# Weight loads that write 128 rows, gate and up blocks paired, and a new order in a one-core attention and feed-forward kernel

## Chip, core and metric

The kernel runs on one core of a Trainium2 chip. The metric is the time of one execution on the device in microseconds (us). The kernel before has a median of 236.81 us over three runs (236.5 to 237.31).

## What is computed

The input x has 2048 rows of 448 numbers (bf16). Its rows are normalised, and the normalised xn feeds two branches. The reference, cut to what matters:

```
xn = layernorm(x)
# branch A: attention in 4 segments of 512 rows, 16 heads of 28, with a memory from segment to segment
q, k, v = xn @ wq, xn @ wk, xn @ wv
for s in range(4):
    p   = softmax(q_s @ k_s.T * 28**-0.5 + causal mask)
    o_s = g * (phi(q_s) @ M) / (phi(q_s) @ z + 1e-6) + (1 - g) * (p @ v_s)
    M  += phi(k_s).T @ v_s ;  z += sum(phi(k_s))
s = o @ wo
# branch B: feed-forward, 448 -> 1792 -> 448
b = (gelu(xn @ w_gate) * (xn @ w_up)) @ w_down
out = x + s * silu(b)
```

## The kernel before, in words

The work goes by segments of 512 rows, in the order attention 0, gate and up 0, attention 1, gate and up 1, and so on; the down product of a segment is done during the attention of the next. 448 is three and a half times 128, so each contraction over 448 is cut into seven chunks of 64 rows. TensorE works on two 64-row halves at once: a matmul on rows 0 to 63 and one on rows 64 to 127 alternate, for two different outputs. Therefore each weight that is contracted with xn stands twice over: in `wqk_sb` wq lies in rows 0 to 63 and wk in rows 64 to 127; in `wgu_sb` the gate weights lie in rows 0 to 63 and the up weights in rows 64 to 127. xn, transposed, is kept in two tiles: `xnT`, and `xS` with the two halves exchanged (`swapped`, L709 and L711: two DMAs from SBUF to SBUF).

`gate_up` (L1183 on) makes one block of 128 hidden columns at a time, 14 blocks a segment: 14 matmuls (L1195), eight that read `xnT` and then six that read `xS`, alternately for the gate bank and the up bank. ScalarE then applies gelu (L1200) and VectorE multiplies by the up bank into `hT` (L1205).

The loads are written with `load` (L592), each one DMA instruction on the queue of SyncE (SP) or ScalarE (ACT). They come in this order: x of segment 0 (`x0`), wq and wk, x of segment 1 (`x1`), wv, x of segment 2 (`x2`), then gate and up in six pieces (L616): four, four and six blocks, each piece 64 rows by 7 chunks by 512 or 768 columns. Later come `wo_in` (L658, 28 rows each) and w_down (L666, 128 rows).

SP also issues all other transfers of the kernel: the DMA transposes of q, k (L870) and xn (L801), the `xS` exchanges, and the transfers that spread the softmax denominators (`den` L998, `dc` L1029, `rdr` L1038, `rb` L1043). SP works in order: an instruction that waits holds those behind it. Each DMA takes one of eight landing semaphores in turn, so it also waits for the landing of the DMA eight before it.

The order on every engine is made when the kernel is built: `arrange` (L371) plays the operations through with estimated durations, picks by the numbers of a table (`PRIO`, and `STEP`, which ties an operation to a step of the attention), and so also decides PSUM banks and who evicts them.

Some names: `wd_sb` holds w_down later, and at first the k and v of segment 0; `kT` and `qT` are the transposed k and q; `pt` are the exponentials of the scores (L1112 ScalarE, scores L1097, product with v L1159); `up0` (L972) is the memory update of segment 0.

Of the kernel before, what the change touches and what calls it, by code (L numbers as in the profile page):

```python
# [1813 lines left out]
```

## Time and profile before

| | |
|---|---|
| median of three runs | 236.81 us |
| the profiled execution: its own time | 237.62 us |
| its span, first to last instruction | 235.9 us |
| mean granted TensorE clock | 0.992 |
| TensorE (PE) busy | 219.2 us, 93% |
| ScalarE (ACT), VectorE (DVE), GpSimd (POOL) busy | 164.9, 157.3, 130.3 us |
| TensorE idle from 0 to 60 us of the span | 10.5 us |
| TensorE busy from 80 to 220 us | 140.0 of 140 us |
| moved by DMA | 27.48 MB, mean 116 GB/s |

The span is what the trace covers; 1.7 us of the execution's time lie around it. The DMA share is the time that packets took, over the 16 DMA engines; it can exceed 1 when packets of one engine overlap. SPq in a row is SP issuing a transfer; where such a row is long, the instruction was held. A DMA's own time is not in that row.

### The profile page before, as it was taken

To read this page: it belongs to the slowest core of one execution; us is meant where nothing else is said; L and a number is where in the kernel's file an instruction comes from. 1 tells how busy PE (TensorE), PEld (TensorE's weight loads), DVE (VectorE), ACT (ScalarE), POOL (GpSimd) and SP (SyncE) were. 2 spreads that over 40 slices of the span, in tenths; PEclk is the share of its full clock that TensorE was granted. 3 is DMA by queue.
4 is the path that set the end of the run, shared out by engine and by line. 5 is a ranking of instruction groups with operands and counts; after the bars stand their busy time and mean duration, and the time that the engine had idled before them with its cause. 6 is when DMAs were issued, how large, how long until landed. Compare 5 with 4: busy or idle time off the path is not lost.

```text
span 235.9 us, 5509 instructions
## 1 busy us (share of the span) xinstructions
PE 219.2 (93%) x2084; PEld 102.8 (44%) x2084; DVE 157.3 (67%) x289; ACT 164.9 (70%) x224; POOL 130.3 (55%) x225
## 2 busy tenths in 40 slices
PE   7786799699999999999999999999999999999990
PEld 4443345244444454444444444445544444445560
DVE  4489499746636998479785676556757795556453
ACT  5596987969469977894397977994769885345120
POOL 5344599600008799971737865314899788054600
PEclk9999999999999999999999999999999999999996
DMA  6999999969940372332669513419056002177011
GB/s 168 227 212 126 189 156 178 165 123 203 262 91 10 68 183 47 90 107 56 167 152 157 144 29 89 76 36 202 27 154 164 3 8 71 47 201 181 1 42 43
DMA packets 43543, 27.48 MB, mean 116 GB/s; under 512 B 28232, under 2 KB 38920, under 8 KB 43512
## 3 DMA queue, kind: packets, MB, share of 16 engines
q1 hardware_dynamic: 42616, 26.43, 55.5%
q10 hardware_dynamic: 896, 0.66, 1.0%
q8 instruction: 17, 0.28, 0.5%
q14 instruction: 14, 0.11, 0.3%
HBM read 16.23 MB, written 2.98 MB: 81 GB/s over the span
## 4 chain that ended last, share of the span: by engine, by line
PE 74%; DMA 7%; SPq 5%; ACT 5%; DVE 4%; issue 2%; POOL 0%; DVEq 0%; ACTq 0%
PE ps L1195 16%; PE ps L1231 16%; PE pp L1195 15%; PE ps L826 11%; PE pp L1097 5%; ACT pt L1112 4%; PE ps L1261 4%; PE ps L1159 4%; DMA x_sb<-in_A_x_dram 4%; SPq L870 3%; DMA wgu_sb<-in_B_w_up_dram 3%; PE ps L1010 1%; PE ps L972 1%; SPq L801 1%; DVE st L750 1%
## 5 line engine op out<-in xcount | busy, mean ns | idle before, releaser
L1112 ACT ACTIVATE pt<-pp 128x1024 bf16<-128x1024 f32 x75 | 73.1, 1028 | 15.5 <-PE pp L1097 15.3
L1123 POOL TENSOR_SCALAR_AFFINE_SELECT pt<-pt 128x256 bf16<-128x256 bf16 x128 | 54.7, 455 | 42.0 <-ACT pt L1112 41.4
L1195 PEld LDWEIGHTS <-wgu_sb 64*128 64x128 bf16 x784 | 38.7, 94 | 49.0 <-issue 4.9
L1231 PE MATMUL ps<-wd_sb,hT 128*128 128x448 bf16 x210 | 43.7, 353 | 0.0
L1195 PE MATMUL pp<-xnT,wgu_sb 64*128 64x512 bf16 x224 | 30.6, 376 | 0.4 <-DMA wgu_sb<-in_B_w_up_dram 0.3
L1195 PE MATMUL ps<-xnT,wgu_sb 64*128 64x512 bf16 x224 | 30.2, 376 | 0.0
L1205 DVE TENSOR_TENSOR hT<-gl,ps 128x512 bf16<-128x512 bf16 x28 | 18.7, 682 | 17.2 <-ACT gl L1200 17.2
L1200 ACT ACTIVATE gl<-pp 128x512 bf16<-128x512 f32 x28 | 16.5, 598 | 19.1 <-PE pp L1195 19.1
L1205 DVE TENSOR_TENSOR hT<-gl,pp 128x512 bf16<-128x512 bf16 x28 | 18.9, 682 | 14.9 <-ACT gl L1200 14.5
L1231 PEld LDWEIGHTS <-hT 128*128 128x128 bf16 x210 | 19.1, 98 | 19.6 <-issue 4.1
L1021 POOL TENSOR_TENSOR om<-om,rb 128x512 f32<-128x512 f32 x12 | 14.8, 1263 | 21.5 <-DMA rb<-rdr 21.5
L1195 PE MATMUL pp<-xS,wgu_sb 64*128 64x512 bf16 x168 | 24.7, 376 | 2.1 <-DMA xS<-xnT 2.1
L1200 ACT ACTIVATE gl<-ps 128x512 bf16<-128x512 f32 x28 | 16.4, 598 | 12.8 <-PE ps L1195 12.1
L1195 PE MATMUL ps<-xS,wgu_sb 64*128 64x512 bf16 x168 | 24.1, 376 | 0.0
L1068 POOL TENSOR_TENSOR oT<-oa,om 128x512 bf16<-128x512 f32 x12 | 15.4, 1294 | 7.9 <-DVE oa L1065 7.9
L943 POOL TENSOR_SCALAR e<-e 128x896 bf16<-128x896 bf16 (+1 forms) x12 | 12.4, 1037 | 9.8 <-ACT e L938 9.4
L826 PE MATMUL ps<-wqk_sb,xnT 64*128 64x448 bf16 x116 | 15.2, 351 | 1.8 <-DMA wqk_sb<-in_A_wk_dram 1.1
L995 DVE COPY oa<-ps 128x512 f32<-128x512 f32 x16 | 10.7, 685 | 6.2 <-PE ps L1159 5.4
L826 PEld LDWEIGHTS <-xnT 64*128 64x128 bf16 x192 | 8.9, 94 | 12.9 <-issue 6.3
L1252 POOL TENSOR_TENSOR oo<-sg,x_sb 128x448 bf16<-128x448 f32 x12 | 13.3, 1115 | 0.3 <-POOL e L943 0.2
L1097 PE MATMUL pp<-qT,kT 32*128 32x384 bf16 (+3 forms) x186 | 12.9, 300 | 0.2 <-ACT pt L1112 0.2
L1261 PE MATMUL ps<-wo_sb,oT 128*128 128x448 bf16 x52 | 11.7, 353 | 0.0
(134 smaller groups left out, 316.5 us busy)
## 6 DMA issues: line engine op xcount, KB each, us to landing
rb<-rdr SPq DMA_DIRECT2D x28, 256.0 KB
xS<-xnT SPq DMA_DIRECT2D x14, 192.0 KB
out_dram<-oo SPq DMA_DIRECT2D x15, 112.0 KB
wd_sb<-in_B_w_down_dram SPq DMA_DIRECT2D x2, 784.0 KB
x_sb<-in_A_x_dram SPq DMA_DIRECT2D x3, 448.0 KB
wgu_sb<-in_B_w_gate_dram SPq DMA_DIRECT2D x2, 448.0 KB
wgu_sb<-in_B_w_up_dram SPq DMA_DIRECT2D x2, 448.0 KB
rdr<-dc SPq DMA_DIRECT2D x28, 32.0 KB
```

The source lines that it names most:

```text
L826: nc.tensor.matmul(out=self.bank.ap()[:, 0:D], lhsT=chunk(self.xT, self.xt, h, self.hi)[:, n * P:(n + 1) * P], rhs=self.w[side[self.hi], h ...
L1021: oU[s, g, 1] = t, gps(f"sm{s}{g}", 1.22, lambda t=t, r=r: nc.gpsimd.tensor_tensor(out=t.ap(), in0=t.ap(), in1=r.ap(), op=ALU.mult), deps= ...
L1068: oT[s][1].append(gps(f"cb{s}{g}", 1.22, lambda g=g, t=t, tm=tm: nc.gpsimd.tensor_tensor(out=dst.ap()[:, g, :], in0=t.ap(), in1=tm.ap(), o ...
L1097: nc.tensor.matmul(out=S2[i // 2].ap(i % 2)[:, c0:c0 + n], lhsT=kT[s][0].ap()[r, g, kb * P:(kb + 1) * P], rhs=qT[s][0].ap()[r, g, kb * P:L ...
L1112: nc.scalar.activation(out=dst, in_=src, func=ACT.Exp, scale=scale)
L1123: nc.gpsimd.affine_select(out=v, in_=v, pattern=[[0, 2], [1, P]], compare_op=ALU.is_ge, fill=0.0, base=0, channel_multiplier=-1)
L1195: nc.tensor.matmul(out=bf.ap(i), lhsT=wgu_sb[side[i], h, cols], rhs=chunk(xT, xt, h, i), start=k == 0, stop=k == NH - 1)
L1200: a = act(f"ge{s}{fc}", L, lambda bf=bf, gl=gl: nc.scalar.activation(out=gl.ap(), in_=bf.ap(0), func=ACT.Gelu_apprx_tanh), func="gelu", de ...
L1205: nc.vector.tensor_tensor(out=hT[s][0].ap()[:, fc, :], in0=gl.ap(), in1=bf.ap(1), op=ALU.mult), deps=[a] + held,
L1231: nc.tensor.matmul(out=bank.ap()[:, 0:D], lhsT=hT[s][0].ap()[:, fc, b * P:(b + 1) * P], rhs=wd_sb[:, fc, :], start=(fc == 0), stop=(fc == ...
L1252: o = op(f"fa{s}{b}{h}", eng, lambda: (nc.vector if o.on == "DVE" else nc.gpsimd).tensor_tensor(out=oo.ap()[:, r], in0=t.ap()[:, r], in1=x ...
L1261: nc.tensor.matmul(out=bank.ap()[:, 0:D], lhsT=oT[s][0].ap()[:, g, b * P:(b + 1) * P], rhs=wo_sb[:, g, :], start=(g == 0), stop=(g == G - 1))
```

## The change

Seven things are changed.

1. The gate and up weights get a tile each, `wg_sb` and `wu_sb`, of 7 chunks by 896 columns. Rows 0 to 63 hold hidden blocks 0 to 6, rows 64 to 127 blocks 7 to 13. One load brings one 64-row chunk of one weight for all 1792 columns: it writes 128 rows of 896 columns (224 KB). There are 14 such loads, in turn gate and up.
2. `gate_up` makes block f and block f+7 of the gate together, then the same two of up. A gate product therefore needs all seven gate loads, where before the first four blocks needed only the first gate piece and the first up piece.
3. wv is loaded in two transfers of 128 rows by three chunks and two of 64 rows by one chunk. Its chunks stand one place further in the lower half of the rows (`(h - self.hi) % NH`), and its product needs all four loads.
4. wq and wk are written with one loop; what is loaded, by which queue and in which order stays as it was.
5. The planner starts its engines at `BEGIN` rather than at 0, and has other estimates for loads, for the check of the norms (`nrm`, `nrm2`) and for `ca`.
6. Each half of a gate or up product has a bank of its own to choose, where before gate and up of a block took a pair of banks.
7. `PRIO` and `STEP` are new throughout, and with them the order on every engine.

```diff
+BEGIN = {"PE": 0.9, "ACT": 0.82, "DVE": 0.93, "POOL": 0.8, "SP": 0.81}
...
-    "wd_in1": 469, "wg0": 310, "wg4": 308, "wg8": 128, "wk0": 445, "wk1": 753, "wo0": 668,
...
-    free = {e: 0.0 for o in ops for e in o.eng}
+    free = dict(BEGIN)
...
-        wgu_sb = const.tile([P, NH, F], BF16, name="wgu_sb")
+        wg_sb = const.tile([P, NH, F // 2], BF16, name="wg_sb")
+        wu_sb = const.tile([P, NH, F // 2], BF16, name="wu_sb")
...
-        wv_in = weight("SP", "wvl", wv_sb, 0, A_wv, [slice(0, NH)]) + weight("SP", "wvh", wv_sb, 1, A_wv, [slice(0, NH)])
+        wv_in = [load("SP", f"wv{k}", wv_sb[:, k:2 * NC3:2, :], A_wv[k * HALF:k * HALF + NC3 * P, :].rearrange(
+            "(c p) n -> p c n", p=P), 336) for k in range(2)]
+        wv_in += [load("SP", f"wv{i + 2}", wv_sb[side[i], NH - 1, :], A_wv[r, :], 56) for i, r in enumerate(
+            (slice(NC3 * P, D), side[0]))]
...
-        gu_in = []
-        for lo, hi in ((0, 4), (4, 8), (8, NFC)):
-            r = slice(lo * P, hi * P)
-            gu_in += [[load("SP", f"{n}{lo}", wgu_sb[side[i], :, r], ap[:, r].rearrange(
-                "(c p) n -> p c n", p=HALF), 112 * (hi - lo)) for i, (n, ap) in enumerate((
-                    ("wg", B_w_gate), ("wu", B_w_up)))]] * (hi - lo)
+        wg_in, wu_in = [], []
+        for h in range(NH):
+            for to, w, ap in ((wg_in, wg_sb, B_w_gate), (wu_in, wu_sb, B_w_up)):
+                to.append(load("SP", f"{'gu'[to is wu_in]}w{h}", w[:, h, :], ap[h * HALF:(h + 1) * HALF, :].rearrange(
+                    "p (i n) -> i p n", i=2), 224, 0.6))
...
+                    prev = pe(f"{'gu'[j]}g{s}{f}", [L] * NH, mm, mode="r64", deps=xd + xe + (wg_in, wu_in)[j],
+                              after=[prev or att.get("sc_end")], prio=at(ph, 2 * f + j) + 0.5, acq=bs, uses=[xT, xt])
```

In the access pattern of the new gate and up loads (`"p (i n) -> i p n"`) the DRAM side counts 2, then 64, then 896 columns; the SBUF side counts 128 rows of 896.

The first place is SP's queue from the load of `x2` on. Before (`wd_sb<-wd_sb` are the transposes of the k of segment 0 into `kT`; `xS_97` is the exchange for the projections of segment 1):

```order
L592 DMA x_sb_65<-in_A_x_dram 128x4x448
L592 DMA wgu_sb<-in_B_w_gate_dram 64x7x512
L592 DMA wgu_sb<-in_B_w_up_dram 64x7x512
L870 DMA_TRANSPOSE wd_sb<-wd_sb 128x4x128 x3
L709 DMA xS_97<-xnT_94 64x1536
L711 DMA xS_97<-xnT_94 64x1536
L592 DMA wgu_sb<-in_B_w_gate_dram 64x7x512
L801 DMA_TRANSPOSE xnT_95<-xn_92 128x4x128 x2
```

After, the same queue from the fifth gate or up load to the exchange `xS_98` for segment 1, with the semaphore that each waits for:

```order
L596 DMA wg_sb<-in_B_w_gate_dram 128x1x896 [waits DMAHW1_49]
L596 DMA wu_sb<-in_B_w_up_dram 128x1x896 [waits DMAHW2_49]
L596 DMA wg_sb<-in_B_w_gate_dram 128x1x896 [waits DMAHW3_49]
L876 DMA_TRANSPOSE wd_sb<-wd_sb 128x4x128 [waits DMAHW4_49,Activation_49,Pool_49]
L876 DMA_TRANSPOSE wd_sb<-wd_sb 128x4x128 [waits DMAHW5_49,Activation_49]
L596 DMA wu_sb<-in_B_w_up_dram 128x1x896 [waits DMAHW6_49]
L876 DMA_TRANSPOSE wd_sb<-wd_sb 128x4x128 [waits DMAHW7_49,DVE_49]
L596 DMA wg_sb<-in_B_w_gate_dram 128x1x896 [waits DMAHW0_49]
L596 DMA wu_sb<-in_B_w_up_dram 128x1x896 [waits DMAHW1_49]
L664 DMA wo_sb<-in_A_wo_dram 28x4x448 [waits DMAHW2_49,Pool_49]
L664 DMA wo_sb<-in_A_wo_dram 28x4x448 [waits DMAHW3_49]
L715 DMA xS_98<-xnT_95 64x1536 [waits DMAHW4_49,DVE_49]
```

Before, two gate and up pieces stand ahead of the three transposes; now seven loads do, and three more stand ahead of the exchange for segment 1.

The second place is the same queue, later. Before, from the last gate piece to the first `den` (the last up piece comes after eight more transposes and an exchange, not shown):

```order
L592 DMA wgu_sb<-in_B_w_gate_dram 64x7x768
L870 DMA_TRANSPOSE qT_98<-e_103 128x4x128
L709 DMA xS_96<-xnT_95 64x1536
L711 DMA xS_96<-xnT_95 64x1536
L998 DMA den_149<-oa_112 4x512
```

After, from the last three gate and up loads to the exchange `xS_97`, which the gate and up of segment 0 read:

```order
L596 DMA wg_sb<-in_B_w_gate_dram 128x1x896
L807 DMA_TRANSPOSE xnT_96<-xn_93 128x4x128 x3
L596 DMA wu_sb<-in_B_w_up_dram 128x1x896
L807 DMA_TRANSPOSE xnT_96<-xn_93 128x4x128
L596 DMA betac<-in_A_beta_dram 128x1x1
L664 DMA wo_sb<-in_A_wo_dram 28x4x448
L715 DMA xS_97<-xnT_96 64x1536
L717 DMA xS_97<-xnT_96 64x1536
```

Now every gate and up load stands ahead of this exchange, and the last of them ahead of the fourth transpose of xn.

The third place is TensorE around its first gate product. Before (`pp1_87` is a pair of banks):

```order
L972 MATMUL ps3_91<-wd_sb_72 128x128
...
L1159 MATMUL ps2_90<-pt0_106,wd_sb_72 32x512
...
L1097 MATMUL pp0_86<-hT_81,wd_sb_72 128x384
...
L1195 MATMUL pp1_87<-xnT2_95,wgu_sb_71 128x512
...
L1195 MATMUL pp1_87<-xS0_96,wgu_sb_71 128x512
```

After:

```order
L1103 MATMUL ps1_90<-hT_82,wd_sb_73 128x128
...
L1203 MATMUL pp1_88<-xnT2_96,wg_sb_71 128x512
...
L1203 MATMUL pp1_88<-xS0_97,wg_sb_71 128x512
...
L978 MATMUL ps0_89<-wd_sb_73 128x128
...
L1165 MATMUL ps3_92<-pt0_107,wd_sb_73 32x512
```

The memory update `up0` (L978) and a product with v (L1165) stood ahead of the gate products and now stand behind the first three of them. The sum of TensorE's rows is the same (5627).

More of the change, by code (lines that the diff above doesn't have):

```diff
@@ L445, in fast_path @@
     NFC = F // P
+    FH = NFC // 2
     NC3 = D // P
@@ L589, in fast_path, with load @@
         first = []
-        def load(eng, name, dst, src, kb, rate=320.0):
-            o = op(name, {eng: (0.5, 2.0)}, lambda: (nc.sync if eng == "SP" else nc.scalar).dma_start(
-                out=dst, in_=src), after=first[-1:], prio=-1000, kb=kb, rate=rate)
+        def load(eng, name, dst, src, kb, occ=0.68):
+            o = op(name, {eng: (occ, 1.45)}, lambda: (nc.sync if eng == "SP" else nc.scalar).dma_start(
+                out=dst, in_=src), after=first[-1:], prio=-1000, kb=kb, rate=335.0)
             first.append(o)
@@ L597, in fast_path, with rows64 @@
         side = slice(0, HALF), slice(HALF, P)
-        def weight(eng, name, dst, hi, ap, parts):
-            v = ap.rearrange("(c p) n -> p c n", p=HALF)
-            return [load(eng, f"{name}{k or ''}", dst[side[hi], c, :], v[:, c, :], len(range(*c.indices(NH))) * ap.shape[1] / 8, 300.0)
-                    for k, c in enumerate(parts)]
-        x0 = [load(e, f"x0{lo}", xs[0][:, lo:hi, :], x_v[0][:, lo:hi, :], 112 * (hi - lo))
+        def rows64(ap):
+            return ap.rearrange("(c p) n -> p c n", p=HALF)
+        x0 = [load(e, f"x0{lo}", xs[0][:, lo:hi, :], x_v[0][:, lo:hi, :], 112 * (hi - lo), 0.45)
               for e, lo, hi in (("SP", 0, 1), ("ACT", 2, 4), ("SP", 1, 2))]
@@ L826, in product @@
                 nc.tensor.matmul(out=self.bank.ap()[:, 0:D], lhsT=chunk(self.xT, self.xt, h, self.hi)[:, n * P:(n + 1) * P],
-                                 rhs=self.w[side[self.hi], h, :], start=k == 0, stop=k == NH - 1)
+                                 rhs=self.w[side[self.hi], (h - self.hi) % NH if self.nm == "wv" else h, :], start=k == 0, stop=k == NH - 1)
             def out(self, o):
@@ L892, in pair @@
             else:
-                f = pe(name, [D] * NC3, mm(0, NC3), deps=[u.w_in[0], v.w_in[0]] + xd, prio=pr, **kw)
-                o = pe("r" + name, [D] * (NH - NC3), mm(NC3, NH), mode="r64", deps=[f, u.w_in[1], v.w_in[1]] + xe,
+                f = pe(name, [D] * NC3, mm(0, NC3), deps=(u.w_in if u.nm == "wv" else [u.w_in[0], v.w_in[0]]) + xd, prio=pr, **kw)
+                o = pe("r" + name, [D] * (NH - NC3), mm(NC3, NH), mode="r64", deps=[f, u.w_in[-1], v.w_in[-1]] + xe,
                        prio=pr - 0.5, uses=[u.bank, v.bank, u.xT])
@@ L1185, in gate_up @@
             (xT, xd), (xt, xe) = xnT[s], xS[s, "g"]
-            hT[s] = [Buf(hT_p), []]
-            prev = a = None
-            for fc in range(NFC):
-                bf, cols = Buf(B_, ANY), slice(fc * P, (fc + 1) * P)
-                def mm(bf=bf, cols=cols):
-                    for k in range(NH):
-                        for i in range(2):
-                            h = turn_of[i][k]
-                            nc.tensor.matmul(out=bf.ap(i), lhsT=wgu_sb[side[i], h, cols], rhs=chunk(xT, xt, h, i),
-                                             start=k == 0, stop=k == NH - 1)
-                o = prev = pe(f"gu{s}{fc}", [L] * 7, mm, mode="r64", deps=xd + xe + gu_in[fc],
-                              after=[prev or att.get("sc_end")], prio=at(ph, fc) + 0.5, acq=[bf], uses=[xT, xt])
-                gl = Buf(gl_p)
-                a = act(f"ge{s}{fc}", L, lambda bf=bf, gl=gl: nc.scalar.activation(
-                    out=gl.ap(), in_=bf.ap(0), func=ACT.Gelu_apprx_tanh), func="gelu", deps=[o],
-                    after=list(tabled), prio=at(ph, fc) - 400, acq=[gl], uses=[bf])
-                held = [att[0][-1]] + qT[0][1] + seg0 if s == 0 else []
-                m = dve(f"hm{s}{fc}", psum_t(L), lambda bf=bf, gl=gl, fc=fc:
-                        nc.vector.tensor_tensor(out=hT[s][0].ap()[:, fc, :], in0=gl.ap(),
-                                                in1=bf.ap(1), op=ALU.mult), deps=[a] + held,
-                        after=hT[s][1][:1], prio=at(ph, fc) - 400,
-                        acq=[] if hT[s][1] else [hT[s][0]],
-                        uses=[gl, bf] + ([hT[s][0]] if hT[s][1] else []))
-                hT[s][1].append(m)
@@ new lines, in gate_up, with mm @@
+            hT[s] = [Buf(hT_p), [None] * NFC]
+            prev = a = first = None
+            for f in range(FH):
+                cols, banks, done = slice(f * P, (f + 1) * P), [], []
+                for j, w in enumerate((wg_sb, wu_sb)):
+                    bs = [Buf(B_) for _ in range(2)]
+                    def mm(w=w, bs=bs, cols=cols):
+                        for k in range(NH):
+                            for i in range(2):
+                                h = turn_of[i][k]
+                                nc.tensor.matmul(out=bs[i].ap(), lhsT=w[side[i], h, cols], rhs=chunk(xT, xt, h, i),
+                                                 start=k == 0, stop=k == NH - 1)
+                    prev = pe(f"{'gu'[j]}g{s}{f}", [L] * NH, mm, mode="r64", deps=xd + xe + (wg_in, wu_in)[j],
+                              after=[prev or att.get("sc_end")], prio=at(ph, 2 * f + j) + 0.5, acq=bs, uses=[xT, xt])
+                    banks.append(bs)
+                    done.append(prev)
+                for i in range(2):
+                    fc, gl, (gb, ub) = f + i * FH, Buf(gl_p), (banks[0][i], banks[1][i])
+                    a = act(f"ge{s}{fc}", L, lambda gb=gb, gl=gl: nc.scalar.activation(
+                        out=gl.ap(), in_=gb.ap(), func=ACT.Gelu_apprx_tanh), func="gelu", deps=[done[0]],
+                        after=list(tabled), prio=at(ph, 2 * f) - 400 + i, acq=[gl], uses=[gb])
+                    held = [att[0][-1]] + qT[0][1] + seg0 if s == 0 else []
+                    m = dve(f"hm{s}{fc}", psum_t(L), lambda ub=ub, gl=gl, fc=fc:
+                            nc.vector.tensor_tensor(out=hT[s][0].ap()[:, fc, :], in0=gl.ap(),
+                                                    in1=ub.ap(), op=ALU.mult), deps=[a, done[1]] + held,
+                            after=[first], prio=at(ph, 2 * f) - 400 + i, acq=[] if first else [hT[s][0]],
+                            uses=[gl, ub] + ([hT[s][0]] if first else []))
+                    hT[s][1][fc] = m
+                    first = first or m
@@ L1336, in both @@
                                      rhs=red, start=True, stop=True)
-            o = pe("nrm", [256], both, deps=last + ones_in, prio=pr, acq=[bank])
+            o = pe("nrm", [570, 570], both, deps=last + ones_in, prio=pr, acq=[bank])
             def fin():
```

12 lines of the change are left out of this document (7 added, 5 removed), and 550 rows, old and new, of tables (PRIO, STEP).

## The prediction

> **What bounds the kernel now.** I read the page first: the busy slices and the chain that ended last. Each digit is a fortieth of the span, 5.9 us.
>
> ```profile
> PE   7786799699999999999999999999999999999990
> DMA  6999999969940372332669513419056002177011
> PE 74%; DMA 7%; SPq 5%; ACT 5%; DVE 4%; issue 2%; POOL 0%; DVEq 0%; ACTq 0%
> ```
>
> From the ninth slice on TensorE is hardly ever short of work until the last products are done; only the first 60 us have holes, and there the DMA engines are full. The table of TensorE's waits names the holes:
>
> ```profile
> PE pp L1195 <- DMA xS<-xnT: 2.1, 2, 1.4
> PE ps L826 <- DMA wv_sb<-in_A_wv_dram: 0.8, 1, 0.8
> PE pp L1195 <- DMA wgu_sb<-in_B_w_up_dram: 0.3, 1, 0.3
> ```
>
> These 3.2 us are all that waits for the loads and exchanges that the change rewrites; the rest of the kernel is TensorE's own work. So the change can win about 3 us at most, and it can lose as much as it delays the first gate product. That product starts here, in TensorE's timeline, and the chain shows where the last of its kind in segment 0 ends:
>
> ```profile
> 45.73 0.80 PE L1195 MATMUL pp<-xS,wgu_sb 64*128 64x512 bf16 x5 [1.36 <-DMA xS<-xnT]
> ...
> 40.14 1.00 PE ps L972 x16
> 41.14 0.69 PE ps L1159 x16
> ...
> 64.62 3.04 PE pp L1195 x28
> ```
>
> From the landing of the exchange at 45.73 to 67.66 (64.62 + 3.04) are 21.9 us, nearly all matmuls.
>
> **The load itself: how many engines carry it.** The new loads are meant to be wider, and the windows of the trace show what width is worth: from 10 to 19 the pieces that write 64 rows are on the way, from 59 to 62 w_down, which writes 128 (last column GB/s).
>
> ```profile
> 10.00:19.00 9.00, 6.95 (x74) 4.11 (x72) 6.53 (x17) 6.99 (x12) 3.78 (x8) 1.00 1.15 210
> 59.00:62.00 3.00, 3.00 (x32) 1.36 (x28) 2.33 (x4) 1.65 (x4) 0.00 (x0) 1.00 1.10 340
> ```
>
> 340 against 210 GB/s speaks for the change. [...]
>
> But the 340 are 16 engines together, 21.3 each, and not every transfer has 16. A transfer of `den` counts four rows on both sides. In the DMA view from 188 to 189.5 us it is alone:
>
> ```profile
> DMA packets 8, 0.01 MB, mean 5 GB/s; under 512 B 4, under 2 KB 4, under 8 KB 8
> q1 hardware_dynamic: 8, 0.01, 1.8%
> den<-oa SPq DMA_DIRECT2D x1, 8.0 KB
> ```
>
> Eight packets: four rows of 2 KB and four of a few bytes, the posts by which an engine reports. Four engines, then, not 16. The page's queues agree:
>
> ```profile
> q1 hardware_dynamic: 42616, 26.43, 55.5%
> q10 hardware_dynamic: 896, 0.66, 1.0%
> ```
>
> q10 is ACT's: its four transfers have 832 rows (256, 256, 192 and 128), so 64 posts, 16 each. On SP's q1 the shapes in the code make 39408 rows, which leaves 3208 posts. 112 transfers with 16, 39 transposes with 32, 28 `den` with 4 and the four `wo_in` of 28 rows with 14 make exactly 1792 + 1248 + 112 + 56 = 3208; were it 16 for every copy, the transposes would have 23.2 each. So the number of engines divides the outermost count: 28 rows get 14, not 16. The new gate and up loads count 2 outermost in DRAM and 128 in SBUF. No row of this trace has a count under 16 on one side only. The bounds are 2 engines (the smaller side decides) and 16 (the SBUF side does). I take 2: each engine's share has to be cut from both lists at once, and a list of two can only be cut in two.
>
> [...]
>
> **The price of one load.** 224 KB on two engines is 229376 B / 2 = 114688 B for each. Slices of the view from 54 to 63 us show the rate of the 896-byte rows of w_down, from 307 to 387 in the filled part:
>
> ```profile
> GB/s 177 218 253 300 307 246 232 205 212 185 199 172 194 193 180 199 219 203 239 247 350 327 331 335 327 339 387 307 327 331 354 331 350 358 335 354 324 315 280 200
> ```
>
> At 340 one engine gives 21.3 GB/s and a load takes 5.4 us; at 387 it gives 24.2 and takes 4.7. The lone `den` took 1.8% of 16 engines for 1.5 us, 0.43 us for four rows of 2 KB: 0.108 us a row, 0.094 for 1792 B, 6.0 us for 64 rows, which is the dear end, since a lone row pays its start. The new rows are twice as long as w_down's, so I take 4.8, near the fast end.
>
> **Who queues behind them.** An engine takes a queue's transfers in turn. The view from 7 to 19 us shows it: SP issued three transposes in that time (from 14.64, timeline), 1536 packets of 256 B, and almost none had moved by 19, because x2, gate and up stood ahead; they moved in the next microsecond.
>
> ```profile
> DMA packets 2877, 2.56 MB, mean 214 GB/s; under 512 B 148, under 2 KB 2877, under 8 KB 2877
> wd_sb<-wd_sb SPq DMA_TRANSPOSE x3
> ...
> 14.64 5.62 SPq L870 DMA_TRANSPOSE wd_sb<-wd_sb  x3
> ...
> 19.00:20.00 1.00, 1.00 (x18) 0.71 (x17) 0.89 (x4) 0.76 (x2) 1.00 (x1) 1.00 3.97 174
> 20.00:21.00 1.00, 1.00 (x14) 0.40 (x11) 0.97 (x4) 0.73 (x2) 0.20 (x1) 1.00 0.51 28
> ```
>
> So whatever SP issues later has its sixteenth on the two loaded engines and lands when they come to it. SP itself is held too, by the landing eight places before, as it is now at the first gate piece (2.50 us for an issue that else takes 0.6):
>
> ```profile
> 3.17 0.61 SPq L592 DMA_DIRECT2D x_sb<-in_A_x_dram  x1
> 6.83 2.50 SPq L592 DMA_DIRECT2D wgu_sb<-in_B_w_gate_dram  x1
> ...
> 3.17 8.81 DMA x_sb<-in_A_x_dram
> ...
> 227.56 1.67 DMA out_dram<-oo
> ```
>
> Now the two engines' day. The load of x1 lands at 11.98 (3.17 + 8.81) as before, nothing ahead of it being changed. Behind it wv and x2, 1.26 MB at 340, take 3.7; a small transfer lands 1.67 after its issue (the last store), so less that the gate loads begin at about 14.0. Each transpose costs an engine about 0.5 (the three above were through in some 1.5 us from 19.0), the pieces of `xS` and `wo` between the loads about 1.5 in all. Seven loads end at 47.6; two transposes of segment 0's k follow, 48.6; up 3, 53.4; the third transpose, 53.9; gate 4 and up 4, 63.5; `wo` and the exchange for segment 1, 65.0; gate 5, up 5, gate 6, 79.4; three transposes of xn, 80.9; up 6, 85.7; the fourth, 86.2. It lands 1.7 later, 87.9, and only then can the exchange for gate and up go out: two issues of about 0.5 and 0.6, landing 1.7 after the second begins: 90.1.
>
> Checked for something later: the second scores need the third transpose (lands 55.6), and the projections of segment 1 need their exchange (66.7). From the first projection of segment 1 to the gate took 15.4 us before, by the first lines of these two products,
>
> ```profile
> 26.80 1.08 PE L826 MATMUL ps<-wqk_sb,xnT 64*128 64x448 bf16 x8
> 42.22 1.04 PE L1195 MATMUL pp<-xnT,wgu_sb 64*128 64x512 bf16 x8
> ```
>
> so TensorE is there at 82, and waits for 90.1. From then on it does what it did from 45.73 to 67.66, and in addition `up0` and one product with v, 1.00 + 0.69, which stood ahead before, less the wait of 0.3 for the last up piece: 1.4.
>
> **The sum.** 90.1 − 45.73 + 1.4 = 45.8 us later at the end of gate and up of segment 0. Nothing gives it back: behind 67.66 TensorE is full. The profiled execution took 237.62, so 283.4; it lies 0.8 above the median of 236.81, so 282.6 there. I say 283.
>
> The other edits have one answer. wv in 128 rows saves its 0.8 us wait only where TensorE then waits for nothing else; here it is lost in the hole. The pairing of f and f+7 keeps 196 matmuls a segment of the same length. The banks, the planner's new estimates and the norm check cost nothing in themselves. The new order past segment 0 I price at 0. What it could win there is bounded by the waits that are left to TensorE, of which the largest is
>
> ```profile
> PE pp L1097 <- ACT pt L1112: 1.6, 4, 0.6
> ```
>
> 1.6 us, and part of that lies ahead of 60 us; what it could lose is of the same size, were scores to wait for an exponential once more. Work on the other engines is hidden under TensorE from 60 us on; without that cover it would cost a us or two.
>
> **The rivals.**
>
> *16 engines after all, faster (0.09).* The SBUF side's 128 decides. Then the 14 loads take 3.2 MB / 340 = 9.4 us, every one of them stands ahead of its use, and the 3.2 us of waits go: 236.8 − 3.2 = 233.6. For it: `rb` and `rdr` have unequal sides (16 and 128) and 16 posts. Against: 16 divides both.
>
> *16 engines, but slower (0.03).* The first gate product now needs all seven gate loads and the second all seven of up. Eight loads more have to be issued, and the last up load stands behind them. Now the last up piece goes out here:
>
> ```profile
> 50.49 1.26 SPq L801
> ...
> 51.80 6.56 DMA wgu_sb<-in_B_w_up_dram
> ```
>
> Eight transposes of 1.26 that stand ahead of it come behind it in the new order: 41.7; eight issues of 0.6 come on top: 46.5; it lands 1.67 + 0.7 later, 48.9. It decides from 43.7, when TensorE begins the second product (42.22 + 1.5): 5.2 us late, less the 3.2 of waits that go: 236.8 + 2.0 = 238.8. Against: most of those issues can go out early, while TensorE still projects.
>
> *Two engines, another pair each time (0.03).* Then seven loads run side by side, each 4.8 us long, and the whole is bound by SP's issues as now: 237.
>
> **How the numbers follow.** My forecast has 0.85: the counts of `den` and `wo_in` show the division, and only unequal sides are unseen. Its ends: with 6.0 a load it is 14 × 1.2 = 16.8 dearer, 300; with a rate above every slice (26 GB/s an engine, 4.4) 5.6 cheaper, 277, and with the rival's 3.2 and a start 3 us earlier on top, 271. From 270 to 302 hold about 0.8 of the chance, since the rivals' 0.15 lie below. Within 0.3% counts as the same, which is about what a measurement of this kernel can tell: faster 0.09, same 0.03, slower 0.88.
>
> **What would show it.** Right: a DMA share near 2 of 16 from 15 to 85 us and some 40 to 50 GB/s; SP issues held for about 5 us each; TensorE waiting for `kT` or scores until about 55, for `xS` of segment 1 until about 67, and for `xS` of segment 0 until about 90, then full to the end. Wrong: GB/s near 300 from 14 to 25 us and the gate product at 42; then the first rival holds. If the DMA share is low, but the gate starts near 80 or 100, the mechanism holds and the 4.8 was the wrong size.

## The result, and the profile after

The changed kernel takes 292.56 us (median of four runs, 291.61 to 293.71), the kernel before 236.94 in runs beside it: a ratio of 1.235, with an interval from 1.23 to 1.24. The prediction was 283.0, with a range from 270 to 302. The profiled execution took 291.61 us, 54.0 more than the one before (237.62); 289.9 of it are the span. Some executions of a kernel ran longer than its others (272.3 us beside 265.75 to 268.1 for only up split below); every median here leaves them out, and a kernel whose profiled execution was one of them has no mark in the table below.

The page after: TensorE, its granted clock, the DMA share and the rate in fortieths of the span (7.25 us), the engines' shares of the chain that ended last, and SP's queue.

```profile
PE   7840000749607999899999899999988999999992
PEclk9985555586955999999999999999999999999999
DMA  6811197411995559353125955233156300262411
GB/s 187 241 48 48 48 65 76 126 45 60 53 101 112 91 131 234 70 138 83 23 62 153 146 151 121 76 78 79 25 135 179 102 21 3 57 179 64 112 33 37
PE 66%; SPq 19%; DMA 8%; DVE 3%; issue 1%; ACT 1%; DVEq 0%; ACTq 0%
q1 hardware_dynamic: 41684, 26.43, 45.3%
```

Where about 200 GB/s and a share of 9 stood, the third to fifth slice (14.5 to 36 us) show 48 GB/s and a share of 1 (0.13 from 24 to 33 us, which is 2.1 of the sixteen engines): two engines, 24 GB/s each. q1 has 932 packets fewer than before. With two posts for each of the 14 loads that is exact: the loads had 2688 rows and 6 x 16 posts before, 1792 rows and 14 x 2 posts now, 964 fewer; wv has the same 896 rows and 32 posts more. Had each load 16 posts, q1 would have lost 736.

SP's issues in the timeline (start, how long the issue was held):

```profile
24.02 4.63 SPq L596 DMA_DIRECT2D wu_sb<-in_B_w_up_dram  x1
28.69 4.63 SPq L596 DMA_DIRECT2D wg_sb<-in_B_w_gate_dram  x1
33.45 9.19 SPq L876 DMA_TRANSPOSE wd_sb<-wd_sb  x2
...
66.82 12.06 SPq L807 DMA_TRANSPOSE xnT<-xn  x3
...
81.58 0.60 SPq L596 DMA_DIRECT2D betac<-in_A_beta_dram  x1
...
87.42 0.53 SPq L715 DMA_DIRECT2D xS<-xnT  x1
```

One load goes out every 4.67 us (24.02 to 28.69), and the transposes are held by the landings before them. TensorE's waits say who stood for it, and its timeline says when:

```profile
PE ps L1103 <- DMA wd_sb<-wd_sb: 32.5, 1, 32.5
PE pp L1103 <- ACT pt L1118: 12.0, 1, 12.0
PE ps L832 <- DMA xS<-xnT: 4.4, 2, 3.8
```

```profile
52.05 0.50 PE L1103 MATMUL ps<-hT,wd_sb 32*128 32x384 bf16 x2 [32.51 <-DMA wd_sb<-wd_sb]
...
65.95 1.30 PE L832 MATMUL ps<-wqk_sb,xS 64*128 64x448 bf16 x5 [0.58 <-DMA xS<-xnT]
...
88.90 0.61 PE L1103 MATMUL pp<-hT,wd_sb 32*128 32x512 bf16 x2 [12.00 <-ACT pt L1118]
...
92.72 1.70 PE L1203 MATMUL pp<-xnT,wg_sb 64*128 64x512 bf16 x8
...
94.25 0.81 PE L1203 MATMUL pp<-xS,wg_sb 64*128 64x512 bf16 x6
...
118.77 0.39 PE L1103 MATMUL pp<-qT,kT 32*128 32x512 bf16 x2 [0.92 <-ACT gl L1211]
```

The reader is to see three holes, each behind a transfer in SP's queue: the transposes of k, the exchange for segment 1, and then 12.0 us named after ScalarE. ScalarE had been idle itself; its own timeline shows what it stood for, the load of beta, which stands behind every gate and up load in SP's queue:

```profile
87.64 0.20 ACT L683 ACTIVATE igate<-betac 128x1 f32<-128x1 bf16 x1 [12.93 <-DMA betac<-in_A_beta_dram]
```

The last row of TensorE's timeline gives a mark that all the changed kernels have: gate and up of segment 0 are done, and the first two scores of segment 1 (0.3 us more), when TensorE begins the wait ahead of the next two, at 118.77 - 0.92 = 117.85. Before has no such wait; there the end of gate and up is taken, 67.66. So 50.2 us are lost up to there, and 3.8 us behind it: 289.9 - 117.85 = 172.05 against 235.9 - 67.66 = 168.24. TensorE's waits behind the mark, of after and then of before, are that 3.8 (4.0 less 0.2):

```profile
PE pp L1203 <- ACT gl L1211: 2.4, 2, 1.2
PE pp L1103 <- ACT gl L1211: 0.9, 1, 0.9
PE pp L1203 <- DVE hT L1216: 0.7, 1, 0.7
```

```profile
PE pp L1097 <- ACT pt L1112: 0.2, 1, 0.2
```

### The profile page after: what moved, and what is told of

It reads as the page before. It is cut to its first block, busy times and chain, and to the rows that moved or that the text cites. A ratio compares the mean times of both kernels' runs of the same rounds, so it can differ in the third digit from the quotient of the medians.

```text
span 289.9 us, 5509 instructions
## 1 busy us (share of the span) xinstructions
PE 225.3 (78%) x2084; PEld 102.7 (35%) x2084; DVE 154.4 (53%) x290; ACT 168.8 (58%) x228; POOL 128.5 (44%) x226
## 3 DMA queue, kind: packets, MB, share of 16 engines
q1 hardware_dynamic: 41684, 26.43, 45.3%
## 4 chain that ended last, share of the span: by engine, by line
PE 66%; SPq 19%; DMA 8%; DVE 3%; issue 1%; ACT 1%; DVEq 0%; ACTq 0%
PE pp L1203 15%; PE ps L1203 14%; PE ps L1242 12%; SPq L596 10%; PE ps L832 8%; SPq L876 4%; PE pp L1103 4%; PE ps L1272 4%; DMA xS<-xnT 4%; PE ps L1165 4%; SPq L807 3%; DMA wqk_sb<-in_A_wk_dram 2%; DMA betac<-in_A_beta_dram 2%; PE pp L1242 1%; SPq L664 1%
## 5 line engine op out<-in xcount | busy, mean ns | idle before, releaser
L1242 PE MATMUL ps<-wd_sb,hT 128*128 128x448 bf16 x182 | 38.4, 353 | 0.0
L1203 PEld LDWEIGHTS <-wg_sb 64*128 64x128 bf16 x392 | 19.4, 95 | 26.9 <-issue 5.1
L1203 PEld LDWEIGHTS <-wu_sb 64*128 64x128 bf16 x392 | 19.9, 94 | 22.7 <-issue 1.6
L1103 PE MATMUL ps<-hT,wd_sb 32*128 32x384 bf16 (+3 forms) x16 | 2.6, 398 | 32.5 <-DMA wd_sb<-wd_sb 32.5
L1118 ACT ACTIVATE pt<-ps 128x512 bf16<-128x512 f32 x14 | 7.6, 599 | 32.2 <-PE pp L1103 31.9
L1203 PE MATMUL ps<-xnT,wu_sb 64*128 64x512 bf16 x120 | 22.7, 376 | 0.0
L1203 PE MATMUL pp<-xnT,wg_sb 64*128 64x512 bf16 x112 | 19.2, 391 | 3.2 <-ACT gl L1211 2.4
L1203 PE MATMUL pp<-xnT,wu_sb 64*128 64x512 bf16 x104 | 20.5, 376 | 0.3 <-ACT gl L1211 0.3
L1203 PE MATMUL ps<-xnT,wg_sb 64*128 64x512 bf16 x112 | 18.5, 377 | 0.0
L1203 PE MATMUL ps<-xS,wu_sb 64*128 64x512 bf16 x90 | 17.9, 376 | 0.0
```

The source lines that it names most:

```text
L1103: nc.tensor.matmul(out=S2[i // 2].ap(i % 2)[:, c0:c0 + n], lhsT=kT[s][0].ap()[r, g, kb * P:(kb + 1) * P], rhs=qT[s][0].ap()[r, g, kb * P:L ...
L1118: nc.scalar.activation(out=dst, in_=src, func=ACT.Exp, scale=scale)
L1203: nc.tensor.matmul(out=bs[i].ap(), lhsT=w[side[i], h, cols], rhs=chunk(xT, xt, h, i), start=k == 0, stop=k == NH - 1)
L1242: nc.tensor.matmul(out=bank.ap()[:, 0:D], lhsT=hT[s][0].ap()[:, fc, b * P:(b + 1) * P], rhs=wd_sb[:, fc, :], start=(fc == 0), stop=(fc == ...
```

## The experiments

Two questions were put: is it the count of engines that makes the 50 us, against the order of the queue or the size of a transfer; and what are the 8 us that the prediction lacked.

| kernel | median, us | ratio to before | mark (gate and up of segment 0 done) | from the mark to the end |
|---|---|---|---|---|
| before | 236.94 | | 67.66 | 168.2 |
| after | 292.56 | 1.235 | 117.85 | 172.05 |
| split into 64-row halves | 248.12 | 1.054 (1.044 to 1.064) | 74.60 | 171.7 |
| split by columns | 297.06 (one run) | | 123.44 | 171.9 |
| only up split | 267.64 | 1.133 (1.122 to 1.144) | | |
| after, beta first | 294.61 | 1.25 (1.239 to 1.262) | 120.80 | 171.9 |
| after, beta first, TensorE kept busy | 298.23 | 1.267 (1.260 to 1.274) | 119.73 | 176.7 |
| after, up loads on ACT's queue | 294.91 (one run) | | 117.87 | 175.3 |
| split, two moves | 251.04 | 1.064 (1.057 to 1.072) | 78.04 | 172.4 |
| split, four gelu buffers | 248.63 | 1.059 (1.052 to 1.065) | 73.37 | 171.7 |
| split, moves and buffers | 249.60 | 1.059 (1.054 to 1.064) | 77.20 | 172.2 |
| 8 gathered halves | 243.73 | 1.030 (1.024 to 1.035) | 70.04 | 171.8 |
| gathered, two ahead | 246.01 | 1.037 (1.031 to 1.044) | 72.91 | 172.5 |
| gathered, two ahead, four buffers | 246.34 | 1.046 (1.040 to 1.052) | 71.90 | 170.9 |

The marks come from each kernel's one profiled execution, as above. Each ratio is to runs of before beside it. The kernels were measured on several chips, so a difference of a us or two between two rows is not clear of noise by the medians alone. For three kernels (TensorE kept busy; split, two moves; split, four gelu buffers) the comparison with before counts as unclear, though their intervals lie above 1.05.

**The same bytes with 64 rows outermost.** Each load becomes two transfers; the order is that of after on every engine.

```diff
-w[:, h, :], ap[h * HALF:(h + 1) * HALF, :].rearrange("p (i n) -> i p n", i=2)
+[w[r, h, :] for r in side], [ap[h * HALF:(h + 1) * HALF, i * FH * P:(i + 1) * FH * P] for i in range(2)]
```

> The changed kernel with one thing undone: each of the 14 gate/up loads is issued as two transfers, 64 rows of block f and 64 rows of block f+7, from the same place in the order, so that 64 rows and not 2 halves are the outermost count on both sides. Order, layout and all other instructions stay. Theory (a load whose outermost count is 2 runs on two DMA engines): the pair of halves takes 0.7 to 0.8 us of the sixteen engines instead of the 4.68 us measured of one load, some 55 us leave the queue, the transfers for the gate of segment 0 are issued before 47 us instead of at 87.4, DMA shows 250 GB/s or more where it showed 48, and the time is 233 to 241 us: 237 if the new order costs nothing, 241 if the 4 us that the changed kernel loses after the gate of segment 0 belong to the order. Rival (the order of the queue, with the loads ahead of the kT transposes, is what holds TensorE, whatever the loads' rate): over 260 us.

Measured: 248.12 us, 44.4 less than after. q1 counts what it should with 16 posts for each half, 28 x 80 in place of 14 x 130, 420 more than the 41684 of after:

```profile
q1 hardware_dynamic: 42104, 26.43, 45.7%
```

The rate, in slices of 6.16 us, is 214 GB/s in the third (12 to 18 us), where after has 48 from 14.5 us on:

```profile
GB/s 171 298 214 140 180 169 104 125 88 88 171 210 83 149 94 22 71 110 134 128 135 128 149 43 72 72 24 147 122 188 40 20 4 59 130 118 174 3 39 44
```

So the two engines are shown to cost 43 to 44 us (the mark moves from 117.85 to 74.60), and the rival, over 260, is out. But the time is 7 us above the upper end of the expectation: the rest, 11 to 12 us, is not the two engines. TensorE's waits in this kernel:

```profile
PE pp L1103 <- ACT pt L1118: 4.3, 1, 4.3
PE ps L1103 <- DMA wd_sb<-wd_sb: 3.9, 2, 3.6
PE pp L1203 <- ACT gl L1211: 2.7, 3, 1.2
```

The same places as in after, only shorter: exponentials behind beta, the transposes of k, and gelu.

**Two transfers, still two halves outermost.** Each load in two pieces of 448 columns.

```diff
+[w[:, h, c:c + 448] for c in (0, 448)], [ap[...].rearrange("p (i n) -> i p n", i=2)[:, :, c:c + 448] for c in (0, 448)]
```

> The changed kernel with each of the 14 loads issued as two transfers of 128 rows by 448 columns: as many transfers and bytes per transfer as in the kernel with 64-row halves, but the outermost count on the DRAM side stays 2. Theory: still two engines, 46 to 49 GB/s, each half held 2.3 to 2.4 us, time 291 to 297 us. Rival (the size of one transfer, or its 128 rows in one piece, makes it slow): smaller transfers cure it, under 260 us.

Measured: 297.06 us in its one run, and the page's rate shows what two engines give with rows of 896 B, 46 GB/s:

```profile
GB/s 191 229 46 46 46 59 77 47 123 46 61 82 99 91 80 290 53 124 109 26 71 102 122 151 149 118 58 92 17 132 127 132 34 17 53 152 83 119 32 37
```

As many transfers as in the split kernel, 49 us slower. Neither the size of a transfer nor the number of them is the cause; the outermost count is.

**Half of the loads split.** Only the up loads, in the way of the first experiment.

> The changed kernel with only the 7 up loads split into 64-row halves; the 7 gate loads stay as they are. Theory: the cost goes by the count of two-engine loads, 7 x (4.68 - 0.75) = 27.5 us less on the queue than in the changed kernel, so the transfers for the gate of segment 0 are issued near 60 us instead of 87.4, and the time is 292.5 - 27.5 = 265 us, from 260 to 270. Rival (the end is set by a single wait that any such load makes, or the kT wait alone): over 280; (most of the seven is hidden by other work): under 250.

Measured: 267.64 us (ratio 1.133), in the expected range. Seven loads cost 267.64 - 248.12 = 19.5 us and the next seven 24.9: about 3.2 us for each load, which goes out 3.4 us later than its two halves do (4.67 against 1.23 us for the pair of issues). The cost goes roughly by the count.

**Beta ahead of the gate loads**, in after. One instruction moves in SP's queue.

> The changed kernel with the 0.2 KB load of beta issued ahead of the first gate load instead of behind the last up load; all else in its order. Theory (the last scores of segment 0 wait 12.0 us for exponentials that stand behind ScalarE's gates, which wait for beta): that wait goes, the 3.8 us of scores and projection that ran from 88.9 to 92.7 us run before 87 us, and the gate of segment 0 begins when its own transfers land, near 88 to 89 us: 3.5 to 5 us less, 288 us, from 287 to 290. Rival (TensorE then only waits for the same transfers, and the low clock after the longer hole takes it back): 291.5 to 293. Rival (the 12.0 us are the bound by themselves): 280 to 283.

Measured: 294.61 us, 2 us slower than after (the intervals of the two ratios just touch). The theory fell, and so did the rival that took the 12.0 us for the bound; the other rival had the right mechanism and a size that was too small. The 12.0 us wait is gone, but TensorE then stands for the gate's own data:

```profile
87.41 1.89 PE L1203 MATMUL pp<-xnT,wg_sb 64*128 64x512 bf16 x8 [7.87 <-DMA xnT<-xn]
...
91.12 1.97 PE L1203 MATMUL pp<-xS,wg_sb 64*128 64x512 bf16 x6 [1.82 <-DMA xS<-xnT]
...
94.55 2.39 PE L1203 MATMUL ps<-xnT,wu_sb 64*128 64x512 bf16 x8 [1.46 <-DVE qs L849]
```

The gate begins 5.3 us sooner and ends 3.0 later (120.80). The windows of 90 to 100 us, of after and then of this kernel, point to the clock (the first number after the length is TensorE's busy time, the third from the end its granted clock):

```profile
90.00:100.00 10.00, 10.00 (x106) 4.51 (x106) 5.95 (x12) 8.72 (x13) 6.06 (x12) 0.80 0.53 93
```

```profile
90.00:100.00 10.00, 7.42 (x31) 2.57 (x32) 4.80 (x10) 1.09 (x2) 0.00 (x0) 0.50 0.47 97
```

In after the scores that were late kept TensorE busy without a break from 88.90 on, and the clock came back at 94. Here TensorE kept stopping (the three waits above), and the clock stayed at half until 100.7. The forecast had 23.3 us from the landing of this exchange to the end of gate and up; here they are 29.7 (120.80 - 91.12).

**The same, with TensorE kept busy in the hole.** 56 matmuls, whose results are overwritten, ahead of the gate's first.

```diff
+[nc.tensor.matmul(out=bs[j % 2].ap()[:, 0:D], lhsT=wqk_sb[side[j % 2], 0, 0:P], rhs=wqk_sb[side[j % 2], 1, :], start=True, stop=True) for j in range(56)]
```

> The changed kernel with beta first (294.6 us) and 56 matmuls more (64 rows, 448 columns, about 0.12 us each, their results overwritten) put in front of the first gate matmul of segment 0, where TensorE stood 7.9 us waiting for transposes. Theory (beta first gained nothing because the longer hole brought the granted clock down to 0.50 from 90 to 100 us, where it was 0.80 with the hole later): with TensorE busy through most of the hole the clock stays above 0.8 there, the first eight gate matmuls take 1.0 to 1.2 us instead of 1.89, and the time falls to 289 us, from 287.5 to 291. Rival (the clock does not follow TensorE's own idle time, or the start of the gate is held by VectorE and ScalarE): 293 to 297.

Measured: 298.23 us, above the ranges of both the theory and the rival. The clock did what the theory said, until 88.7 (1.00 in every window of 1 us from 84 to 88, where with beta first alone it is 0.50), and with the next waits it is at 0.50 again, until 98.9:

```profile
87.42 1.04 PE L1203 MATMUL pp<-xnT,wg_sb 64*128 64x512 bf16 x8 [1.79 <-DMA xnT<-xn]
90.13 0.58 PE L1203 MATMUL pp<-xS,wg_sb 64*128 64x512 bf16 x1 [1.67 <-DMA xS<-xnT]
...
94.24 2.39 PE L1203 MATMUL ps<-xnT,wu_sb 64*128 64x512 bf16 x8 [1.70 <-DVE qs L849]
```

The first eight take 1.04 us instead of 1.89, the eight of up 2.39 at a clock of 0.50, and the mark is 1.1 us sooner than without (119.73). The time is longer all the same, because 4.8 us more are lost behind the mark. Most of that can be read. TensorE's waits behind the mark are 7.1 us instead of 4.4, and behind one of them, for gelu in segment 1's gate, the clock is down once more:

```profile
166.96 1.72 PE L1203 MATMUL pp<-xnT,wg_sb 64*128 64x512 bf16 x8 [2.03 <-ACT gl L1211]
```

```profile
160.00:170.00 10.00, 7.97 (x62) 3.51 (x60) 8.99 (x20) 6.25 (x8) 3.45 (x4) 0.86 0.66 145
```

The same wait is 1.63 us with beta first alone and 1.24 in after, and there the clock is 1.00 from 160 to 180. Here the means are 0.86 from 160 to 170 and 0.97 from 170 to 180, so by estimate it is at half for 3.4 us (to 170.6), which is some 1.7 us lost; with 2.7 of longer waits that is 4.4 of the 4.8. Why the waits are longer, long after the added matmuls, was not found. So the experiment shows a higher clock in the hole with TensorE at work (1.00 against 0.50 from 84 to 88), and not that this work saves time.

**The up loads on ACT's queue**, still with two halves outermost.

```diff
-(nc.sync if eng == "SP" else nc.scalar).dma_start(
+(nc.sync if eng == "SP" and name[:2] != "uw" else nc.scalar).dma_start(
```

> The changed kernel with the seven up loads issued by ScalarE instead of SP, in two-engine form as before; the gate loads stay on SP. Theory (a transfer whose outermost count is 2 goes to the same two of the sixteen engines whichever queue issues it): from 15 to 60 us DMA still shows 46 to 50 GB/s, and the time is 280 to 300 us. Rival (each queue has a pair of its own, or pairs rotate): 90 to 98 GB/s while both load, and the time is 255 to 275 us. ScalarE's own work can be held behind its issues, which makes the time a weaker reading than the GB/s.

Measured: 294.91 us. The DMA view from 15 to 35 us, while both queues load:

```profile
DMA packets 547, 0.98 MB, mean 49 GB/s; under 512 B 6, under 2 KB 546, under 8 KB 546
q1 hardware_dynamic: 289, 0.51, 7.1%
q10 hardware_dynamic: 257, 0.46, 6.1%
```

49 GB/s in all, half for each queue, and 13.2% of 16 engines, which is two; after shows 48 GB/s and 13.2% in the same window with one queue. The second queue adds no engine; the rival with a pair for each queue is out. The mark is that of after; of the 3.3 us more behind it 1.4 are again waits (5.4 us against 4.0, the longest 2.0 for gelu). The granted clock of the whole run is 0.887 against 0.898; where behind the mark it was lower was not shown.

**Moves in the split kernel's queue.** Beta first, and four loads behind a transpose of k.

> The kernel with split loads (248.1 us), with two moves in SP's queue: beta's load ahead of the first gate load, and gate and up loads 2, gate load 3 and up load 3 behind the three kT transposes of segment 0. All else, order of the other engines included, stays. Theory (with 16-engine loads, what is left before the end of segment 0's gate and up is the new order of SP's queue: a wait of 3.6 us for kT and one of 4.3 us for exponentials behind beta, 6.6 us at the end of that gate, 74.25 us against 67.66 in the kernel before): both waits go, 248.1 - 6.6 = 241.5 us, from 239.5 to 243. Rival (the waits only move, as with beta first in the changed kernel, to the transfers of segment 0's gate and to VectorE): 246 to 249.

Measured: 251.04 us, 2.9 slower than the split kernel instead of 6.6 faster, and above the rival's range too. The edit did not do what it was meant to: the operation behind which the loads were put was the first of the three transposes to go out, not the last, so that two came even later and TensorE waited 5.8 us for them.

```profile
16.28 1.31 SPq L876 DMA_TRANSPOSE wd_sb<-wd_sb  x1
...
22.80 2.52 SPq L876 DMA_TRANSPOSE wd_sb<-wd_sb  x2
```

What it does show again is the other half, beta first: the 4.3 us for exponentials are replaced by 2.0 for `xS` and 1.8 for `qs`, as the rival said. The theory that both waits simply go is not borne out.

**Four gelu buffers in the split kernel.**

```diff
-gl_p = slots(3, [P, L], BF16, "gl")
+gl_p = slots(3, [P, L], BF16, "gl"); gl4 = gl_p.aps + slots(1, [P, L], BF16, "gx").aps
```

> The kernel with split loads (248.1 us), with four gelu buffers (gl) in turn instead of three; order and all else stay. Theory (gate and up now make f and f+7 together, so that two gl buffers are taken at a time, ScalarE waits for VectorE to give back the third, and TensorE waits 2.4 + 0.9 + 0.7 = 4.0 us on L1211 and L1216 behind the first segment's gate, where the kernel before waits 0.2): four buffers take most of the 4.0 us away, 244 to 245 us. Rival (the order of ScalarE, with its table loads between, sets when gelus run, and the buffers do not): no change, 247 to 249.

Measured: 248.63 us (248.12 without), in the rival's range. The waits behind the mark:

```profile
PE pp L1203 <- ACT gl L1211: 1.2, 1, 1.2
PE pp L1203 <- DVE hT L1216: 0.9, 2, 0.7
PE pp L1103 <- ACT gl L1211: 0.9, 1, 0.9
```

3.0 of the 4.0 us are left: having three buffers is 1.0 of them, and the median does not show even that. The buffers are not the main cause. That it is the banks of f and f+7, held until both are multiplied, is read from the names in the rows (`pp`) and was not tried, nor was the rival's cause, ScalarE's own order.

> Split loads, the moves of the two earlier experiments in SP's queue, and four gelu buffers, all together. Theory (the two-engine loads, the order of SP's queue and the gelu buffers are the whole difference): 248.1 - 6.6 - 4.0 = 237.5 us, from 235 to 240, no different from before. Rival (a part of the new order that none of these touches costs time): above 241.

Moves and buffers together: 249.60 us, the rival's side. With the faulty move in it, this says nothing on whether the three causes are all.

**Fewer, larger transfers of 64 rows.**

```diff
+GR = {0: [(0, 0)], 1: [(1, 0)], 4: [(0, 4)], 5: [(1, 4)]}
+[w[side[i], k:k + 4 - k // 4, :] for i, k in GR.get(h, [])], [ap.rearrange("(c p) n -> p c n", p=HALF)[:, k:k + 4 - k // 4, i * FH * P:(i + 1) * FH * P] for i, k in GR.get(h, [])]
```

> The kernel with split loads, with the same halves gathered into 8 transfers instead of 28: 64 rows of f or of f+7 by four (then three) of the seven 64-row blocks, the first four transfers before the kT transposes, the others at the places of gate and up loads 4 and 5. Same bytes, same 64-row outermost count; beta stays behind the xnT transposes. Background: the kernel with split loads takes 248.1 us; its 28 issues hold SP for 0.6 us each, 17 us in all, and in the first moves of this queue a kT transpose that came later cost 3 us more. Theory (what is left of the new order's price is SP's own issue time: each transpose and xS stands behind 0.6 us for every load issued ahead of it): 20 issues less free 12 us of SP, the kT transposes go out near 15 us instead of 19.4, beta and the transposes of segment 0's gate some 8 us sooner, the holes of 3.6 and 4.3 us shrink to under 2 us, and the time is 242 us, from 239 to 244.5. Rival (the turns wait for data from other engines, not for SP): 247 to 250.

Measured: 243.73 us, 4.4 less than with 28 issues and in the expected range. Beta goes out at 35.56 us instead of 41.78, and the wait for exponentials (4.3) is gone; the one for k is not:

```profile
PE ps L1103 <- DMA wd_sb<-wd_sb: 3.9, 1, 3.9
```

The transposes of k are issued from 13.79 to 20.1 us instead of 19.38 to 24.6, so SP's issue time is one part of what the order costs, and not the part that holds the transposes of k. That wait also costs more than its 3.9 us: the rows behind it, from 24.29 to about 31, are longer (six matmuls of wv on `xS` 1.33 us at 27.50, and 0.73 at 39.26), some 3 us by estimate from these rows. In the split kernel the granted clock is 0.50 from 20 to 30 us, with the same wait at 3.6.

**Half the bytes ahead of the transposes.**

```diff
-GR = {0: [(0, 0)], 1: [(1, 0)], 4: [(0, 4)], 5: [(1, 4)]}
+GR = {0: [(0, 0)], 4: [(1, 0), (0, 4)], 5: [(1, 4)]}
```

> The kernel with 8 gathered transfers (243.7 us), with the second pair of four (448 KB each) put behind the three kT transposes of segment 0 instead of ahead of them, so that 0.9 MB of gate and up stand ahead of the transposes, as in the kernel before, and not 1.8 MB. Theory (the last transpose was issued by 20.1 us and landed near 24.2 because bytes of the loads were still ahead of it): it lands 2 to 4 us sooner, TensorE's wait of 3.9 us falls under 1.5 us, the granted clock does not fall near 24 us, and the time is 240.5 us, from 239 to 242. Rival (the transposes are slow by themselves or wait for their rows, or the time won is lost again in the wait for the transfers of segment 0's gate): 243 to 245.

Measured: 246.01 us, above the ranges of both. The wait for k is gone. In part that is because TensorE comes there 2.3 us later; but in the next kernel, with the same queue, the transposes of k are there at 21.05 us instead of 24.29, though the last of them was issued only 0.3 us sooner, so it was the bytes that held them:

```profile
21.05 0.57 PE L1103 MATMUL ps<-hT,wd_sb 32*128 32x384 bf16 x2 [0.49 <-DMA wd_sb<-wd_sb]
```

Now the exchange for segment 1 stands behind more of the loads, and in this kernel TensorE waits there instead:

```profile
33.63 0.36 PE L832 MATMUL ps<-wqk_sb,xS 64*128 64x448 bf16 x1 [1.77 <-DMA xS<-xnT]
35.21 1.05 PE L832 MATMUL ps<-wqk_sb,xS 64*128 64x448 bf16 x5 [1.23 <-DMA xS<-xnT]
```

The rival's mechanism held: the time won was lost again at the next place in the same queue.

> The kernel of the run before with four gelu buffers. With three, TensorE waited 4.0 us in four places behind segment 0's gate; in the run with four buffers 3.0 us of these were left. Theory (1.0 us of the 4.0 is the third buffer, the rest is the two banks that f and f+7 hold until both are multiplied): 1 us less than the run before, 239.5 us, from 238 to 241, and still above the kernel before. Rival (what the buffer frees is taken by the next wait): no difference between the two.

Measured: 246.34 us with the fourth buffer, against 246.01: no difference, the rival's case. No version tried is faster than the kernel before; the best, with 8 gathered halves, is 3.0% slower.

## Why the prediction was right, and where it was off

**The count of engines: right.** The packet count fits two posts a load to the packet, the split by columns stays at 46 GB/s, the split by rows takes 43 us away. Unequal sides, which no row of before showed, follow the smaller one here: loads that count 2 against 128 ran at 48 GB/s and a share of 0.13. That one load after another takes the same two engines, as the sum has it, was the author's estimate, and no run shows which engines they are; in after it is 48 GB/s from 14.5 to 36 us, with several loads on the way, and 49 with two queues.

**The price of one load: right.** 4.8 us was said, 4.67 measured, 24.5 GB/s an engine.

**The queue: right in kind, off by up to 3.6 us, with errors that cancel.** The third transpose of k was forecast to land at 55.6, and TensorE went on at 52.05. Segment 1's exchange was forecast for 66.7 and TensorE had it at 65.95. The exchange for the first gate was forecast for 90.1; in after nothing shows it, but with beta first TensorE waits for it until 91.12: the fourth transpose was there at 87.4 (87.9 was said), but the exchange took 3.1 us from its second issue and not 1.7.

**"TensorE is there at 82, and waits for 90.1": this step failed.** It stood from 76.9 to 88.90, and for something else: exponentials behind ScalarE's `gates`, behind beta, behind the last load. The prediction followed the two engines' queue for the transposes and exchanges and left out the 0.2 KB load at its end. By itself that cost little. More was the clock, for which the prediction has no term: the scores, the projection and the first eight gate matmuls from 88.90 to 94.25 ran at half the granted clock after the hole, and the first matmul on `xS` came at 94.25, 4.15 us later than forecast. By the spacing of the same rows at full clock they would have taken 2.8 us and not 5.35, so by estimate 2.5 of the 4.15 are the clock, 1.0 the later exchange and 0.6 the work left behind the wait for beta. From there to the mark are 23.6 us (117.85 - 94.25), for which the prediction had 23.3; the 0.3 are the first two scores. That this stretch came off as forecast is luck: with beta first TensorE had nearly the wait that was forecast, and needed 29.7, since the gate itself then ran at half clock (0.50 from 90 to 100 us) and stopped again. In after TensorE was busy with the late scores and the projection from 88.90 on, and the clock was back at 94.10, just before it.

**"The new order past segment 0 I price at 0": this term was mis-sized.** It is 3.8 us, all of it waits for gelu and for `hT` in the paired gate and up, about the same in every kernel that has the pairs. Whether the pairing or the new order makes them was not separated. The time behind the mark shows it (171.7 to 172.5 us in nine of the twelve with a mark; 170.9 in one with four buffers, 175.3 and 176.7 in two with a wait for gelu of 2.0 us among these; split, two moves has such a wait too, and 172.4). The bound of 1.6 us either way came from the largest wait of before, which could not show it: there the gate was made one block at a time. "Then full to the end" was wrong by as much.

The sum as measured: 45.8 + 4.15 + 0.3 + 3.8 = 54.05, and the two profiled executions differ by 54.0. The 283 lies 9.6 us below the 292.56; the range held it because it was wide on the dear side for another reason, a load of 6.0 us.

**The rivals.** The 233.6 us for 16 engines was far off: with 16 engines the kernel takes 248.1, or 243.7 with fewer issues, because the other edits, which the prediction said have one answer, cost 7 to 12 us once the two engines are out of the way (with the 64-row halves that were tried in their place). The rival on the slower side (238.8) had the sign for that case, but the wrong place: not the last up piece, but k's transposes, beta and gelu. The rival with another pair of engines each time is out by the 48 GB/s, one pair's rate, while several loads were on the way.

**What stays open:** what the 2.4 us are made of by which the mark of the gathered kernel is still late (the wait for k and the longer rows behind it are more than that, so something else is shorter than in before), the cause of three of the four waits behind the mark, and why these waits are longer in the kernel that kept TensorE busy and in the one with ACT's queue. One transfer of 128 rows on sixteen engines, which is what the change set out to have, was not tried.

## What to carry to other kernels

Before a transfer is made wider, look at the outermost count of both access patterns: here a pattern that begins with two halves ran at 48 GB/s, and the same rows as two transfers of 64 rows freed 43 us or more. When a queue is late, list everything that stands behind it down to the smallest load, and do not add up its waits: three times here a wait was taken away and came back at the next place in the same queue. And price a hole in TensorE's work with the time at half clock that was seen to follow it: in after the granted clock was still 0.50 for the first 5.2 us of work behind the hole (88.90 to 94.10).
